# First group of a pooled-attention and gelu MLP kernel: half of K pooled on the PE, w_in in 512 KB pieces cast by GpSimd, gelus over two blocks, and 64x64 score tiles for the remainder rows

## The chip, the cores and the metric

The kernel runs on 1 core of one Trainium2 chip. The metric is the device time in microseconds (us) of one execution; medians over several executions are given. The profile of one execution gives a span, from the first to the last instruction, that is shorter than the device time of that execution: by 2.00 to 2.18 us in every run of the kernel before and of what was built from it (299.3 against 301.36 us), but by only 1.67 to 1.79 us in every run of the changed kernel and of what was built from that. So spans are compared with spans and times with times; the result comes back to these 0.3 us.

In the profile's lines PE is TensorE (PEld its weight loads), DVE VectorE, ACT ScalarE, POOL GpSimd and SPq the queue that issues the loads. Of the tiles, kv holds the loaded K and V, sc the scores, e their exponentials, r the reciprocals of the sums, eb the attention weights (e times r; this step is called the norm), tp a transpose, xo the values, xT the MLP's input. w_in_s is the loaded float32 w_in, w_in_b its bfloat16 cast, mm the MLP's result in PSUM, the memory that TensorE writes to, and gT the gelus.

## The reference

```python
def _attn_ref(q, k, v):                      # each (8, 8, 576, 64) float32
    B, H, S, D = q.shape
    pool = 8
    Sp = S // pool                           # 72
    k_p = k.reshape(B, H, Sp, pool, D).mean(axis=3)
    v_p = v.reshape(B, H, Sp, pool, D).mean(axis=3)
    scores = (1 / sqrt(D)) * matmul(q, k_p.T)
    attn = softmax(scores)                   # over the 72 pooled keys
    return matmul(attn, v_p)

def _moe_ref(x, w_in, w_out):                # x (4608, 512), w_in (512, 2048), w_out (2048, 512)
    h = x @ w_in
    g = gelu_tanh(h)
    return g @ w_out
```

The attention output, with its heads side by side, is x. All inputs and the output are float32.

## The kernel before

The rows are worked in nine groups of 512: 512 rows of each batch entry, and one "remainder" group R with the last 64 rows of all eight. A group's MLP is 64 hidden matmuls (w_in is stationary, columns of xT move) with a gelu for each block of 128, then 64 output matmuls. The attention of the next group is slipped in between these matmuls by "hooks", numbered by the matmul ahead of which they stand. In the first group nothing can hide the attention or the loads: it works in two halves of 256 rows, in chunks of four blocks of 128 (one chunk needs 1 MB of w_in).

```python
    def pool(b, c0, c1):                     # eight rows summed on VectorE
        ...
        add(out=t[:, :, 0:4, :], in0=t[:, :, 0:4, :], in1=t[:, :, 4:8, :], op=ALU.add)
        add(out=t[:, :, 0:2, :], in0=t[:, :, 0:2, :], in1=t[:, :, 2:4, :], op=ALU.add)
        add(out=kvb[:, c0:c1, 0, :], in0=t[:, :, 0, :], in1=t[:, :, 1, :], op=ALU.add)

    def pool_v_pe(b, c0, c1, eng):           # or eight matmuls with the identity, in fp32
        ps = psum.tile([128, 2, D], F32, name="vp", tag="mm", bufs=4)
        for i in range(8):
            nc.tensor.matmul(out=ps, lhsT=identf, rhs=st[b]["kv"][:, c0:c1, i, :], start=(i == 0), stop=(i == 7))
        copy(eng, st[b]["kvb"][:, c0:c1, 0, :], ps)
    ...
    def scores(g, j):
        ...
            else:                            # group R: two batch entries share a block of 128 rows
                for half in range(2):
                    p0 = 64 * half
                    nc.tensor.matmul(out=o[p0:p0 + 64], lhsT=qT[:, j, pr, p0:p0 + 64],
                                     rhs=kbd[:, 2 * j + half, pr].rearrange("d hh s -> d (hh s)"),
                                     start=True, stop=True)
    ...
    def hidden(g, fo, c0, c1, hook, s):
        hp = psum.tile([128, MAIN], F32, name="mm", tag="mm", bufs=4)
        for ko in range(KO):
            hook(s + ko)
            nc.tensor.matmul(out=hp[:, 0:c1 - c0], lhsT=w_in_b[:, ko, fo * 128:(fo + 1) * 128],
                             rhs=st[g]["xT"][:, ko, c0:c1], start=(ko == 0), stop=(ko == KO - 1))
        nc.scalar.activation(out=gT[:, fo, c0:c1], in_=hp[:, 0:c1 - c0], func=ACT.Gelu_apprx_tanh)
    ...
        for half, c in [(0, 0), (0, 1), (0, 2), (0, 3), (1, 0), (1, 1), (1, 2), (1, 3)]:   # the first group
            for fo in range(4 * c, 4 * c + 4):
                hidden(g, fo, 256 * half, 256 * half + 256, hook, s)
                s += 4
    ...
    warm_up(44, "mm")                        # filler matmuls for the TensorE clock
    kT_tile(0, "mm")
    pool(0, 0, 2)
    dup_k(0, 0, 2)
    k_transpose_pe(0, 0, 2)
    pool(0, 2, 4)
    dup_k(0, 2, 4)
    warm_up(22, "mm")
    k_transpose_pe(0, 2, 4)
    ...
    norm(0, 2, nc.gpsimd)                    # block 2 of the first group: its multiply on GpSimd
    cast_w_in(1, nc.vector)                  # w_in was loaded in four pieces of 1 MB
    norm(0, 3, nc.vector)
    cast_w_in(2, nc.gpsimd)
```

The softmax here doesn't subtract the row's maximum and nothing guards it: scores larger than these inputs give would overflow.

Of the kernel before, what the change touches and what calls it, by code (L numbers as in the profile page):

```python
# [19 lines left out]
def kernel(  # L20
# [100 lines left out]

    def pool(b, c0, c1):
        if "kvb" not in st[b]:
            st[b]["kvb"] = work.tile([128, NB, 2, D], BF16, name="kvb")
        t = st[b]["kv"][:, c0:c1]
        kvb = st[b]["kvb"]
        add = nc.vector.tensor_tensor
        add(out=t[:, :, 0:4, :], in0=t[:, :, 0:4, :], in1=t[:, :, 4:8, :], op=ALU.add)  # L128
        add(out=t[:, :, 0:2, :], in0=t[:, :, 0:2, :], in1=t[:, :, 2:4, :], op=ALU.add)  # L129
        add(out=kvb[:, c0:c1, 0, :], in0=t[:, :, 0, :], in1=t[:, :, 1, :], op=ALU.add)  # L130

    def pool_v_pe(b, c0, c1, eng):

        ps = psum.tile([128, 2, D], F32, name="vp", tag="mm", bufs=4)
        for i in range(8):
            nc.tensor.matmul(out=ps, lhsT=identf, rhs=st[b]["kv"][:, c0:c1, i, :], start=(i == 0), stop=(i == 7))
        copy(eng, st[b]["kvb"][:, c0:c1, 0, :], ps)

# [63 lines left out]
    def scores(g, j):  # L202
        sc = psum.tile([128, 2, MAIN], F32, name="sc", tag="sc", bufs=2)
        qT = st[g]["qT"]
        for pr in range(HP):
            o = sc[:, pr // 2, 2 * Sp * (pr % 2):2 * Sp * (pr % 2) + 2 * Sp]
            if g < B:
                nc.tensor.matmul(out=o, lhsT=qT[:, j, pr, :], rhs=kbd[:, g, pr].rearrange("d hh s -> d (hh s)"),  # L208
                                 start=True, stop=True)
            else:  # L210
                for half in range(2):
                    p0 = 64 * half
                    nc.tensor.matmul(out=o[p0:p0 + 64], lhsT=qT[:, j, pr, p0:p0 + 64],  # L213
                                     rhs=kbd[:, 2 * j + half, pr].rearrange("d hh s -> d (hh s)"),
                                     start=True, stop=True)
        st[g][("sc", j)] = sc
# [8 lines left out]
    def norm(g, j, eng):  # L225
        e = st[g][("e", j)]
        den = work.tile([128, H], F32, name="den")
        nc.vector.reduce_sum(out=den, in_=e, axis=AX.X)  # L228
        r = work.tile([128, H], F32, name="r")
        nc.vector.reciprocal(out=r, in_=den)  # L230
        eng.tensor_tensor(out=eb[:, j, 128 * 5 - W:].rearrange("p (h s) -> p h s", s=Sp), in0=e,  # L231
                          in1=r.unsqueeze(2).to_broadcast([128, H, Sp]), op=ALU.mult)

    def eT_tile(g):
        st[g]["eT"] = work.tile([128, 4, 5, 128], BF16, name="eT", bufs=1)

    def e_transpose_pe(g, j, eng):
        tp = psum.tile([128, 5, 128], BF16, name="tp", tag="mm", bufs=4)
        for c in range(5):
            nc.tensor.transpose(out=tp[:, c, :], in_=eb[:, j, 128 * c:128 * c + 128], identity=identb)  # L240
        copy(eng, st[g]["eT"][:, j], tp)
# [6 lines left out]

    def values_half(g, half, x, eng):

        xo = psum.tile([128, 2, 256], F32, name="xo", tag="mm", bufs=4)
        for i in range(2):
# [38 lines left out]

    def hidden(g, fo, c0, c1, hook, s):
        hp = psum.tile([128, MAIN], F32, name="mm", tag="mm", bufs=4)
        for ko in range(KO):
            hook(s + ko)
            nc.tensor.matmul(out=hp[:, 0:c1 - c0], lhsT=w_in_b[:, ko, fo * 128:(fo + 1) * 128],  # L296
                             rhs=st[g]["xT"][:, ko, c0:c1], start=(ko == 0), stop=(ko == KO - 1))
        nc.scalar.activation(out=gT[:, fo, c0:c1], in_=hp[:, 0:c1 - c0], func=ACT.Gelu_apprx_tanh)  # L298

# [9 lines left out]
    def mlp(g, hooks, last):  # L309
        hook = runner(hooks)  # L310
        for fo in range(FO):
            hidden(g, fo, 0, MAIN, hook, 4 * fo)
        if not last:
# [21 lines left out]
    def mlp_first(g, hooks):  # L335

        hook = runner(hooks)
        s = 0
        for half, c in [(0, 0), (0, 1), (0, 2), (0, 3), (1, 0), (1, 1), (1, 2), (1, 3)]:
            for fo in range(4 * c, 4 * c + 4):  # L340
                hidden(g, fo, 256 * half, 256 * half + 256, hook, s)
                s += 4
        nc.scalar.preload_act_table_set(EXP_SET)
# [28 lines left out]
    w_in_s = []  # L372
    for c in range(2):
        t = kvp.tile([128, KO, 1024], F32, name="w_in_s", tag="kv")
        w_in_s.append(t)
        for i in range(2):
            nc.sync.dma_start(
                out=t[:, :, 512 * i:512 * i + 512],
                in_=moe_w_in[:, 1024 * c + 512 * i:1024 * c + 512 * i + 512].rearrange("(ko p) f -> p ko f", p=128))

    def cast_w_in(c, eng):
        o = 512 * c
        copy(eng, w_in_b[:, :, o:o + 512], w_in_s[c // 2][:, :, 512 * (c % 2):512 * (c % 2) + 512])

# [7 lines left out]

    def cast_w_out(c, eng):
        copy(eng, w_out_b[:, 4 * c:4 * c + 4, :], w_out_s[c // 2][:, 4 * (c % 2):4 * (c % 2) + 4, :])

    make_identity(nc, identb)
    nc.vector.memset(kbd, 0.0)
    nc.gpsimd.memset(vmask, 0.125)  # L398
# [5 lines left out]
    nc.gpsimd.memset(vbd[0:64, :, 0, :], 0.0)  # L404
    make_identity(nc, identf)

# [5 lines left out]

    warm_up(44, "mm")
    kT_tile(0, "mm")
    pool(0, 0, 2)
    dup_k(0, 0, 2)
    k_transpose_pe(0, 0, 2)
    pool(0, 2, 4)
    dup_k(0, 2, 4)
    warm_up(22, "mm")  # L420
    k_transpose_pe(0, 2, 4)
    pool(0, 4, 5)
    dup_k(0, 4, 5)
    warm_up(22, "mm")
    k_transpose_pe(0, 4, 5)
    k_spread(0, [nc.vector, nc.scalar])
    qT_tile(0)
    eT_tile(0)
    xT_tile(0)
    warm_up(12, "mm")  # L430
    cast_q(0, 0, 1, nc.vector)
    cast_q(0, 1, 2, nc.scalar)
    q_transpose_pe(0, 0, nc.vector, "mm")
    q_transpose_pe(0, 1, nc.scalar, "mm")
    warm_up(4, "sc")
    for j in range(2):
# [3 lines left out]
    spread_v(0, nc.gpsimd, (0,))  # L440
    pool_v_pe(0, 7, 9, nc.scalar)
    spread_v(0, nc.gpsimd, (1,))
    cast_q(0, 2, 4, nc.gpsimd)
    spread_v(0, nc.gpsimd, (2,))
    warm_up(8, "mm")
    norm(0, 0, nc.vector)
    norm(0, 1, nc.vector)
    e_transpose_pe(0, 0, nc.scalar)
    q_transpose_pe(0, 2, nc.scalar, "mm")
    q_transpose_pe(0, 3, nc.scalar, "mm")  # L450
    e_transpose_pe(0, 1, nc.vector)
    cast_w_in(0, nc.vector)
    scores(0, 2)
    exps(0, 2)
    values_half(0, 0, 0, nc.vector)
    scores(0, 3)
    exps(0, 3)
    values_half(0, 0, 1, nc.scalar)
    nc.scalar.preload_act_table_set(GELU_SET)
    norm(0, 2, nc.gpsimd)  # L460
    cast_w_in(1, nc.vector)
    norm(0, 3, nc.vector)
    cast_w_in(2, nc.gpsimd)

    def first_t(j):
        e_transpose_pe(0, j, nc.vector)

    def first_v():
        cast_w_in(3, nc.vector)
        values_half(0, 1, 0, nc.scalar)  # L470
        values_half(0, 1, 1, nc.vector)

# [7 lines left out]
    for c in range(4):  # L480
        w_out_load(c)
    load_main(1, "v", 0, 4, nc.sync)

# [20 lines left out]
    at(hooks, 32, first_t, 3)  # L504
    at(hooks, 42, first_v)
    at(hooks, 66, pool, 1, 0, 4)
    at(hooks, 66, dup_k, 1, 0, 4)
    at(hooks, 66, pool, 1, 4, 5)
    at(hooks, 66, dup_k, 1, 4, 5)
    at(hooks, 80, cast_q, 1, 0, 2, nc.vector)  # L510
    at(hooks, 80, cast_q, 1, 2, 4, nc.vector)
    at(hooks, 96, kT_tile, 1, "sc")
    at(hooks, 96, qT_tile, 1)
    at(hooks, 96, k_transpose_pe, 1, 0, 5)
    at(hooks, 96, k_spread, 1, [nc.vector, nc.vector])
    for j in range(4):
        at(hooks, 104 + 6 * j, q_transpose_pe, 1, j, nc.vector, "sc")
    at(hooks, 122, eT_tile, 1)
    at(hooks, 122, cast_w_out, 0, nc.vector)
    at(hooks, 122, cast_w_out, 1, nc.gpsimd)  # L520
    for j in range(4):
        at(hooks, [126, 127, 136, 140][j], scores, 1, j)
        at(hooks, [128, 128, 136, 140][j], exps, 1, j)
        at(hooks, [136, 140, 144, 148][j], norm, 1, j, nc.vector)
        at(hooks, [136, 140, 144, 148][j], e_transpose_dma, 1, j)
    at(hooks, 141, cast_w_out, 2, nc.scalar)
    at(hooks, 141, cast_w_out, 3, nc.scalar)
    for i in range(2):
        at(hooks, 160, pool, 1, 5 + 2 * i, 7 + 2 * i)
        at(hooks, 160, spread_v, 1, nc.gpsimd, (0, 1) if i == 0 else (2,))  # L530
    at(hooks, 150, q_tile, 2)
    at(hooks, 150, load_q, 2, 0, 4, nc.sync)
    at(hooks, 150, load_kv, 2)
    tail_of_attention(hooks, 1, 187)
    mlp_first(0, hooks)

    for n_, g in enumerate(seq):
# [3 lines left out]
        if n_ + 1 < len(seq):  # L541
# [7 lines left out]
            if kv:  # L549
                t0 = 20 if n_ == 1 else 12  # L550
                at(hooks, t0, pool, b, 0, 5)
# [58 lines left out]
```

## Time and profile before

| | kernel before |
|---|---|
| median of the device time | 301.14 us (300.91 to 301.18) |
| span of the profile | 299.3 us |
| first hidden matmul | 19.26 us |
| first output matmul of the first group | 38.70 us |
| first hidden matmul of the second group | 54.94 us |
| a later group | 30.4 us |

The prediction below shows the page's chain, the two largest groups, the stage windows and PE's waits. What it doesn't show is the chain in order of time (start, us, what), which is the best measure for a comparison, since it has the matmuls whose records are missing filled in:

```profile
20.25 2.09 POOL eb L231
22.34 0.05 issue
22.38 0.45 PE tp L240 x5
22.83 1.75 PE mm L296 x16
...
55.11 13.81 PE mm L296 x64
...
221.33 0.37 PE sc L213 x8
```

The reader should see three marks: GpSimd's multiply on the chain at 20.25, the second group's hidden matmuls from 55.11 (their first record starts at 54.94; the chain is 0.17 later), and a score set of the remainder group of 0.37 us (there are four).

### The profile page before, as it was taken

The page shows a single profiled execution, that of the slowest core. Times are in us where ns is not written, and L with a number is a line of the kernel's source. Part 1 is how long each engine was busy: PE and PEld are TensorE (multiplying, and loading weights), DVE is VectorE, ACT ScalarE, POOL GpSimd, SP SyncE. Part 2 cuts the span into 40 slices and gives each one's busy share as a digit, 9 for nine tenths or more (in the row PEclk, how much of TensorE's full clock was granted, in tenths as well). Part 3 has the DMA queues.
Part 4 walks back from the last instruction along what each step waited for, and adds up shares of the span by engine and source line. Part 5 has one row for each costly group of instructions (what it writes and reads, how often), then busy time and mean ns, then how long its engine had stood idle before and what let it go on. Part 6 is the DMA issues. An engine that isn't in the chain of part 4 may idle for free.

```text
span 299.3 us, 4581 instructions
## 1 busy us (share of the span) xinstructions
PE 290.7 (97%) x1734; PEld 151.6 (51%) x1734; DVE 146.7 (49%) x241; ACT 158.2 (53%) x242; POOL 55.5 (19%) x71
## 2 busy tenths in 40 slices
PE   7869999999999999999999999999999999999996
PEld 7748844445444544454445444544444544444444
DVE  6895769164706570648073807381639100920012
ACT  1477783667157715672477246724773267426500
POOL 3252033230400240024012400240024000100000
PEclk9999999999999999999999999999999999999999
DMA  7999997995699459947993599049944800351012
GB/s 235 357 387 338 384 350 132 343 279 158 135 279 250 145 127 271 269 146 126 261 297 134 119 249 301 4 107 249 276 147 101 164 36 2 79 114 37 0 70 70
DMA packets 73221, 56.32 MB, mean 188 GB/s; under 512 B 45808, under 2 KB 55408, under 8 KB 73200
## 3 DMA queue, kind: packets, MB, share of 16 engines
q1 hardware_dynamic: 73056, 55.98, 68.2%
q8 instruction: 13, 0.21, 0.3%
q10 hardware_dynamic: 144, 0.07, 0.1%
q14 instruction: 8, 0.07, 0.1%
HBM read 36.70 MB, written 9.44 MB: 154 GB/s over the span
## 4 chain that ended last, share of the span: by engine, by line
PE 91%; DMA 3%; DVE 2%; SPq 1%; POOL 1%; issue 0%; POOLq 0%
PE mm L296 41%; PE mm L301 41%; PE xo L266 4%; DMA q_sb<-in_q_dram 3%; PE sc L208 2%; PE mm L329 1%; POOL eb L231 1%; SPq L98 1%; PE xo L272 1%; PE tp L193 1%; PE sc L213 0%; DVE w_in_b L80 0%; PE tp L240 0%; DVE w_out_b L80 0%; POOL q_b L80 0%; PE xo L255 0%
## 5 line engine op out<-in xcount | busy, mean ns | idle before, releaser
L301 PE MATMUL mm<-w_out_b,gT 128*128 128x512 bf16 x560 | 128.6, 379 | 0.5 <-DVE w_out_b L80 0.5
L296 PE MATMUL mm<-xT,w_in_b 128*128 128x512 bf16 (+1 forms) x640 | 127.6, 358 | 0.5 <-DVE xT L80 0.5
L298 ACT ACTIVATE gT<-mm 128x512 bf16<-128x512 f32 (+1 forms) x160 | 88.4, 555 | 47.0 <-PE mm L296 45.9
L296 PEld LDWEIGHTS <-w_in_b 128*128 128x128 bf16 x640 | 62.2, 98 | 62.6 <-issue 0.5
L301 PEld LDWEIGHTS <-gT 128*128 128x128 bf16 x560 | 53.4, 98 | 59.7 <-DVE w_out_b L80 0.7
L80 DVE COPY osb<-mm 128x512 f32<-128x512 f32 (+2 forms) x37 | 24.3, 658 | 62.9 <-PE mm L301 60.8
L78 ACT CAST xT<-xo 128x1024 bf16<-128x1024 f32 (+1 forms) x18 | 16.6, 966 | 56.8 <-PE xo L266 49.1
L228 DVE TENSOR_REDUCE den<-e 128x8 f32<-128x576 f32 x36 | 26.5, 736 | 38.0 <-ACT e L221 37.9
L148 POOL TENSOR_TENSOR vbd<-kvb,vmask 128x256 bf16<-128x256 bf16 (+2 forms) x40 | 21.2, 553 | 113.5 <-DVE kvb L130 113.4
L128 DVE TENSOR_TENSOR kv<-kv 128x1024 f32<-128x1024 f32 (+3 forms) x20 | 22.4, 1118 | 29.7 <-DMA kv<-in_v_dram 27.7
L231 DVE TENSOR_TENSOR eb<-e,r 128x576 bf16<-128x576 f32 x28 | 27.2, 970 | 1.0
L221 ACT ACTIVATE e<-sc 128x576 f32<-128x576 f32 x36 | 22.5, 650 | 9.6 <-ACT e L221 4.0
L231 POOL TENSOR_TENSOR eb<-e,r 128x576 bf16<-128x576 f32 x8 | 10.1, 1266 | 71.5 <-ACT e L221 41.1
L80 POOL CAST q_b<-q_sb 128x2048 bf16<-128x2048 f32 (+1 forms) x7 | 15.0, 2147 | 4.1 <-DMA q_sb<-in_q_dram 4.1
L208 PEld LDWEIGHTS <-qT 128*128 128x128 bf16 x128 | 10.1, 98 | 7.0 <-ACT qT L78 0.6
L208 PE MATMUL sc<-kbd,qT 128*128 128x144 bf16 x128 | 13.2, 226 | 0.2 <-ACT qT L78 0.2
L266 PE MATMUL xo<-eT,vbd 128*128 128x512 bf16 x56 | 13.2, 379 | 0.0
L129 DVE TENSOR_TENSOR kv<-kv 128x512 f32<-128x512 f32 (+3 forms) x20 | 12.8, 640 | 0.7
L410 PE MATMUL warm<-identb 128*128 128x128 bf16 x112 | 9.1, 249 | 1.4 <-POOL vmask L398 1.4
L494 ACT ACT_TABLE_LOAD x8 | 10.3, 1283 | 0.1
L80 DVE COPY kbd<-kTd 64x288 bf16<-64x288 bf16 x12 | 5.6, 467 | 8.3 <-DMA kTd<-kvb 8.2
L314 ACT ACT_TABLE_LOAD x7 | 9.0, 1283 | 0.1
(55 smaller groups left out, 99.5 us busy)
## 6 DMA issues: line engine op xcount, KB each, us to landing
out_dram<-osb SPq DMA_DIRECT2D x31, 256.0 KB, 6.7
kv<-in_k_dram SPq DMA_DIRECT2D x7, 1024.0 KB, 6.5
q_sb<-in_q_dram SPq DMA_DIRECT2D x7, 1024.0 KB, 5.9
kv<-in_v_dram SPq DMA_DIRECT2D x7, 1024.0 KB, 9.9
w_in_s<-in_moe_w_in_dram SPq DMA_DIRECT2D x4, 1024.0 KB, 13.0
w_out_s<-in_moe_w_out_dram SPq DMA_DIRECT2D x4, 1024.0 KB, 13.8
out_dram<-osb SPq DMA_DIRECT2D x9, 128.0 KB, 2.3
kv<-in_k_dram SPq DMA_DIRECT2D x2, 512.0 KB, 3.9
```

What stands on the lines that cost most here:

```text
L78: eng.copy(out=out, in_=in_)
L80: eng.tensor_copy(out=out, in_=in_)
L128: add(out=t[:, :, 0:4, :], in0=t[:, :, 0:4, :], in1=t[:, :, 4:8, :], op=ALU.add)
L148: eng.tensor_tensor(out=vbd[p0:128, b, n0:n1, :].rearrange("p (c r) (hh d) -> p c (r hh) d", c=max(m, 1), d=D), in0=kvb[p0:128, 4 + c0:4 + ...
L208: nc.tensor.matmul(out=o, lhsT=qT[:, j, pr, :], rhs=kbd[:, g, pr].rearrange("d hh s -> d (hh s)"), start=True, stop=True)
L221: nc.scalar.activation(out=e.rearrange("p (x h) s -> p x (h s)", x=2), in_=sc[:, :, 0:4 * Sp], func=ACT.Exp, scale=1.0 / 64.0)
L228: nc.vector.reduce_sum(out=den, in_=e, axis=AX.X)
L231: eng.tensor_tensor(out=eb[:, j, 128 * 5 - W:].rearrange("p (h s) -> p h s", s=Sp), in0=e, in1=r.unsqueeze(2).to_broadcast([128, H, Sp]), ...
L266: nc.tensor.matmul(out=xo[:, i, :], lhsT=vbd[:, g, n, :], rhs=eT[:, :, c, :], start=(x == 0), stop=(x == 1))
L296: nc.tensor.matmul(out=hp[:, 0:c1 - c0], lhsT=w_in_b[:, ko, fo * 128:(fo + 1) * 128], rhs=st[g]["xT"][:, ko, c0:c1], start=(ko == 0), stop ...
L298: nc.scalar.activation(out=gT[:, fo, c0:c1], in_=hp[:, 0:c1 - c0], func=ACT.Gelu_apprx_tanh)
L301: nc.tensor.matmul(out=o, lhsT=gT[:, fo, r * 128:(r + 1) * 128], rhs=w_out_b[:, fo, :], start=(fo == 0), stop=(fo == FO - 1))
```

## The change

The intent: in the first group, get K pooled sooner by sharing the sums between VectorE and PE; load w_in in half-MB pieces and have GpSimd cast each piece as it lands; give VectorE the norm of block 2 instead; put the first chunk of half 1 ahead of chunk 3 in half 0, so that PE has work while the last MB comes; halve the number of gelus; drop 66 of 112 filler matmuls. Two more parts: q's first cast moves ahead of the spreading of K and the second from ScalarE to GpSimd, and the first half of w_out is cast by GpSimd in five smaller pieces (hook 110), where VectorE and GpSimd cast 1 MB each (hook 122). Outside the first group, the remainder's scores use the array as four 64x64 tiles. Cut to its core (hook numbers, loads of the next group, the casts of w_out, the norm's new layout for group R and buffer tags are left out):

```diff
-    def pool_v_pe(b, c0, c1, eng):
-
+    def pool_pe(b, c0, c1, copies, eng):
+
+        n = c1 - c0
         ps = psum.tile([128, 2, D], F32, name="vp", tag="mm", bufs=4)
         for i in range(8):
-            nc.tensor.matmul(out=ps, lhsT=identf, rhs=st[b]["kv"][:, c0:c1, i, :], start=(i == 0), stop=(i == 7))
-        copy(eng, st[b]["kvb"][:, c0:c1, 0, :], ps)
+            nc.tensor.matmul(out=ps[:, 0:n], lhsT=identf, rhs=st[b]["kv"][:, c0:c1, i, :], start=(i == 0), stop=(i == 7))
+        kvb = st[b]["kvb"]
+        copy(eng, kvb[:, c0:c1, 0:copies, :], ps[:, 0:n].unsqueeze(2).to_broadcast([128, n, copies, D]))
...
+            for hh in range(2):
+                for p0 in (0, 64):
+                    h0 = 64 * hh
+                    nc.tensor.matmul(out=sc[p0:p0 + 64, hh, Sp * pr:Sp * pr + Sp],
+                                     lhsT=qT[h0:h0 + 64, j, pr, p0:p0 + 64],
+                                     rhs=kbd[h0:h0 + 64, 2 * j + p0 // 64, pr, hh], start=True, stop=True)
...
+    def hidden_half(g, fo, half, hook, s):
+
+        c0 = 256 * half
+        hp = psum.tile([128, 2, 256], F32, name="mm", tag="mm", bufs=4)
+        for f in range(2):
+            for ko in range(KO):
+                hook(s + 4 * f + ko)
+                nc.tensor.matmul(out=hp[:, f, :], lhsT=w_in_b[:, ko, (fo + f) * 128:(fo + f + 1) * 128],
+                                 rhs=st[g]["xT"][:, ko, c0:c0 + 256], start=(ko == 0), stop=(ko == KO - 1))
+        nc.scalar.activation(out=gT[:, fo:fo + 2, c0:c0 + 256], in_=hp, func=ACT.Gelu_apprx_tanh)
...
-        for half, c in [(0, 0), (0, 1), (0, 2), (0, 3), (1, 0), (1, 1), (1, 2), (1, 3)]:
-            for fo in range(4 * c, 4 * c + 4):
-                hidden(g, fo, 256 * half, 256 * half + 256, hook, s)
-                s += 4
+        for half, c in [(0, 0), (0, 1), (0, 2), (1, 0), (0, 3), (1, 1), (1, 2), (1, 3)]:
+            for fo in range(4 * c, 4 * c + 4, 2):
+                hidden_half(g, fo, half, hook, s)
+                s += 8
...
-    for c in range(2):
-        t = kvp.tile([128, KO, 1024], F32, name="w_in_s", tag="kv")
-        w_in_s.append(t)
-        for i in range(2):
+    for c in range(4):
+        if c % 2 == 0:
+            w_in_s.append(kvp.tile([128, KO, 1024], F32, name="w_in_s", tag="kv"))
+        o = 512 * (c % 2)
+        for k0 in (0, 2):
             nc.sync.dma_start(
-                out=t[:, :, 512 * i:512 * i + 512],
-                in_=moe_w_in[:, 1024 * c + 512 * i:1024 * c + 512 * i + 512].rearrange("(ko p) f -> p ko f", p=128))
-
-    def cast_w_in(c, eng):
-        o = 512 * c
-        copy(eng, w_in_b[:, :, o:o + 512], w_in_s[c // 2][:, :, 512 * (c % 2):512 * (c % 2) + 512])
+                out=w_in_s[-1][:, k0:k0 + 2, o:o + 512],
+                in_=moe_w_in[128 * k0:128 * k0 + 256, 512 * c:512 * c + 512].rearrange("(ko p) f -> p ko f", p=128))
+
+    def cast_w_in(c, k0, eng):
+        o = 512 * (c % 2)
+        copy(eng, w_in_b[:, k0:k0 + 2, 512 * c:512 * c + 512], w_in_s[c // 2][:, k0:k0 + 2, o:o + 512])
...
-    warm_up(44, "mm")
+    kvb_tile(0)
+    qT_tile(0)
+    eT_tile(0)
+    xT_tile(0)
+    warm_up(34, "mm")
     kT_tile(0, "mm")
     pool(0, 0, 2)
     dup_k(0, 0, 2)
+    pool_pe(0, 2, 4, 2, nc.scalar)
     k_transpose_pe(0, 0, 2)
-    pool(0, 2, 4)
-    dup_k(0, 2, 4)
-    warm_up(22, "mm")
-    k_transpose_pe(0, 2, 4)
     pool(0, 4, 5)
     dup_k(0, 4, 5)
-    warm_up(22, "mm")
     k_transpose_pe(0, 4, 5)
+    k_transpose_pe(0, 2, 4)
+    cast_q(0, 0, 1, nc.vector)
     k_spread(0, [nc.vector, nc.scalar])
-    qT_tile(0)
-    eT_tile(0)
-    xT_tile(0)
-    warm_up(12, "mm")
-    cast_q(0, 0, 1, nc.vector)
-    cast_q(0, 1, 2, nc.scalar)
+    cast_q(0, 1, 2, nc.gpsimd)
+    warm_up(4, "sc")
     q_transpose_pe(0, 0, nc.vector, "mm")
     q_transpose_pe(0, 1, nc.scalar, "mm")
-    warm_up(4, "sc")
     for j in range(2):
         scores(0, j)
         exps(0, j)
     pool(0, 5, 7)
     spread_v(0, nc.gpsimd, (0,))
-    pool_v_pe(0, 7, 9, nc.scalar)
+    pool_pe(0, 7, 9, 1, nc.scalar)
     spread_v(0, nc.gpsimd, (1,))
-    cast_q(0, 2, 4, nc.gpsimd)
+    cast_q(0, 2, 3, nc.gpsimd)
     spread_v(0, nc.gpsimd, (2,))
-    warm_up(8, "mm")
     norm(0, 0, nc.vector)
     norm(0, 1, nc.vector)
-    e_transpose_pe(0, 0, nc.scalar)
+    e_transpose_pe(0, 0, nc.scalar, "mm")
+    cast_q(0, 3, 4, nc.scalar)
+    cast_w_in(0, 0, nc.gpsimd)
+    warm_up(8, "sc")
+    e_transpose_pe(0, 1, nc.vector, "mm")
     q_transpose_pe(0, 2, nc.scalar, "mm")
     q_transpose_pe(0, 3, nc.scalar, "mm")
-    e_transpose_pe(0, 1, nc.vector)
-    cast_w_in(0, nc.vector)
-    scores(0, 2)
-    exps(0, 2)
-    values_half(0, 0, 0, nc.vector)
-    scores(0, 3)
-    exps(0, 3)
-    values_half(0, 0, 1, nc.scalar)
+    cast_w_in(0, 2, nc.vector)
+    for x in range(2):
+        values_half(0, 0, x, [nc.vector, nc.scalar][x], "mm")
+    for j in (2, 3):
+        scores(0, j)
+        exps(0, j)
     nc.scalar.preload_act_table_set(GELU_SET)
-    norm(0, 2, nc.gpsimd)
-    cast_w_in(1, nc.vector)
+    norm(0, 2, nc.vector)
     norm(0, 3, nc.vector)
-    cast_w_in(2, nc.gpsimd)
+    for c in range(1, 4):
+        cast_w_in(c, 0, nc.gpsimd)
+        cast_w_in(c, 2, nc.gpsimd)
```

## The prediction

The sum is -1.45 + 0.15 = -1.3 us, giving 299.8 and, with something for the landings, 299.6; its +0.15 was the estimate for the remainder's scores. In step (3), the 1.2 us of a cast beside VectorE's work was an estimate; half of the 2.33 us that GpSimd's cast of 128x2048 took beside VectorE's cast of w_out (alone 1.93) comes to 1.17. Rival B keeps the wait; the causes that it gave, GpSimd's order of work among them, are cut with the delay of 0.5 to 1 us.

> **What bounds the kernel now.** I read the page first. Its chain that ended last, and the costliest two groups:
>
> ```profile
> PE 91%; DMA 3%; DVE 2%; SPq 1%; POOL 1%; issue 0%; POOLq 0%
> L301 PE MATMUL mm<-w_out_b,gT 128*128 128x512 bf16 x560 | 128.6, 379 | 0.5 <-DVE w_out_b L80 0.5
> L296 PE MATMUL mm<-xT,w_in_b 128*128 128x512 bf16 (+1 forms) x640 | 127.6, 358 | 0.5 <-DVE xT L80 0.5
> ```
>
> The chain is 91% PE, so only what lies before or between matmuls can be won. Second view, the windows: before the first hidden matmul, hidden phase of the first group, its output phase, one later group (columns: stretch, length, then busy us of each engine with its count, clock, DMA share, GB/s).
>
> ```profile
> 0.00:19.26 19.26, 15.36 (x183) 13.50 (x184) 14.78 (x29) 7.66 (x13) 6.86 (x19) 1.00 0.95 316
> 19.26:38.70 19.44, 17.75 (x176) 15.43 (x175) 14.71 (x27) 14.09 (x36) 4.64 (x3) 1.00 1.06 367
> 38.70:54.94 16.24, 16.20 (x80) 7.56 (x81) 11.67 (x21) 10.32 (x10) 4.75 (x6) 1.00 0.88 248
> 54.94:85.50 30.56, 30.56 (x154) 14.39 (x153) 14.54 (x25) 17.31 (x26) 7.92 (x8) 1.00 0.84 217
> ```
>
> A later group has no PE gap at all. The hidden phase of the first group loses 19.44 - 17.75 = 1.69 us, the output phase 0.04. Before 19.26 PE works on the attention and on filler. So the change can win only a start before 19.26, those 1.69 us, and what it does to the remainder group's scores. The third view, PE's waits in the first 60 us, names the 1.69 (total, times, longest); the timeline shows what stood behind:
>
> ```profile
> PE tp L240 <- POOL eb L231: 1.2, 1, 1.2
> PE mm L301 <- DVE w_out_b L80: 0.5, 1, 0.5
> ...
> 17.38 1.23 DVE L80 CAST w_in_b<-w_in_s 128x2048 bf16<-128x2048 f32 x1
> 18.53 0.68 DVE L80 CAST xT<-xo 128x512 bf16<-128x512 f32 x1
> 20.25 2.08 POOL L231 TENSOR_TENSOR eb<-e,r 128x576 bf16<-128x576 f32 x1 [3.07 <-DVE r L230]
> 22.83 1.93 POOL L80 CAST w_in_b<-w_in_s 128x2048 bf16<-128x2048 f32 x1 [0.51 <-DMA w_in_s<-in_moe_w_in_dram]
> 25.52 1.23 DVE L80 CAST w_in_b<-w_in_s 128x2048 bf16<-128x2048 f32 x1
> ```
>
> The reader should see two things. GpSimd's multiply of 2.08 us holds the transposes at 22.38. And the casts start when their data land: in the view of tile w_in_s,
>
> ```profile
> L377 SPq DMA_DIRECT2D w_in_s<-in_moe_w_in_dram x4: 1827/1955/2387, 5.4 to 11.3; - x4
> DMA to landing us min/median/max: 11.9/13.0/14.2
> ```
>
> issue plus landing gives 5.4 + 11.9 = 17.3 for the first MB and 11.3 + 14.2 = 25.5 for the last, so one MB each 2.7 us (17.4, 20.1, 22.8, 25.5), with the DMA share at 0.95 to 1.06: **the load of w_in is a second bound, close behind PE**.
>
> [...] VectorE's multiply eb<-e,r took 0.82 us at 13.31 but 1.29 us at 15.06 beside GpSimd, and GpSimd's cast of 128x2048 took 1.93 us alone, 2.33 us beside VectorE's cast of w_out. [...] 44 filler matmuls took 4.45 us from 1.43, the next 22 only 1.39. [...] the trace has 0.42 us of weight-load idle before each set of eight 128x64 score matmuls, and 0.37 us for the set. [...] gelu of 256 columns 385 ns, of 512 about 600.
>
> **The change part by part.**
> (1) K's middle half goes from VectorE to PE: VectorE loses 0.68 + 0.42 + 0.29 + 0.20 = 1.6 us. PE gains eight fp32 matmuls, 2.0 us by the V half that PE already pools; ScalarE a copy of 256 columns, about 0.35. VectorE is done with K at about 7.6 instead of 8.64. But K's transposes of that half wait for landing 5.75 (read from the trace's landing times) + 2.0 + 0.35 = 8.2, and q's first half lands only at 8.6. Scores start near 9.9 instead of 11.14: 1.2 us won, but not yet at the end.
> (2) That lead is then lost to data. q's second half lands at 14.65 in both kernels, and gates the transposes of q; w_in's first MB is complete at 17.36. VectorE now casts only half of it, 0.65 us, done at 18.0; its copy of xT (0.68) follows in order: first hidden matmul near 18.7. **Won at the start: 0.5 us.**
> (3) Seven of eight half-MB casts are GpSimd's, 0.97 us each (half of 1.93), a piece landing each 1.35 us, so it keeps up[...]. The norm of the third block moves to VectorE: e at 18.8, eb at about 20.6 to 21.0. Chunk 0 of hidden work is 16 x 0.11 = 1.76 us, until 20.5, so the wait of 1.19 shrinks to some 0.3. Chunk 1 is cast at 20.07 + 1.2 = 21.3; PE needs it at about 21.3. Chunk 2 is cast at 22.78 + 1.1 = 23.9; PE needs it at 21.3 + 1.76 + 0.45 (transposes) = 23.5. Chunk 3, at 26.6, is now needed only after the first chunk of half 1, at about 28.4: no wait.
> (4) So the landing of chunk 2 sets the phase. From 23.9: rest of chunk 2 1.76, values 1.04, five chunks 8.8, K transposes 0.35, q transposes 4 x 0.22: end 36.75. Before, outputs began at 38.70 after two scores (0.5) that now fall into the output phase: compare with 38.2. **Won in all up to the outputs: 38.2 - 36.75 = 1.45 us**, the 0.5 of (2) included.
> (5) w_out lands in the same order behind the same DMA load (first MB 35.3, then each 2.7 us); GpSimd casts its first 128x512 piece by 35.9, before 36.75. Later pieces: fo 4 needed at 40.7, ready 39; fo 8 needed near 44.6, ScalarE's casts start near 42.3. No wait. V of the next group lands by 46.04, is pooled on VectorE by 49, spread by 49.7; its values come near 50.7. No wait, 1 us spare.
> (6) Gelus over two blocks: ScalarE 16 x 0.60 = 9.6 instead of 32 x 0.385 = 12.3 us, not on the chain: 0.
> (7) Remainder group scores: per block 16 matmuls of 64x64 by 72 columns for 8 of 128x64 by 144. [...]
> Sum: -1.45 + 0.15 = -1.3, giving 299.8; since the author may gain something from smaller landings, I take **299.6 us**.
>
> **The rivals.**
> A. Landings improve: half-MB pieces complete earlier than now because less later data runs ahead of them. For it: by the page's queue rates about 0.9 MB more than its own had moved when each MB landed. Against: total bytes and rate are unchanged. Worth up to 1 us at chunk 2: 298.5.
> B. A new wait takes the place: [...] PE waits for GpSimd's w_in_b instead of eb. For it: seven casts beside VectorE's norms. Against: 0.97 us per 1.35. It makes 300.3 to 301.
> C. The clock: fillers fall from 112 to 46 matmuls, so PE could fall back to half clock before 19 us. For it: PE would be thin between 13.9 and 15.4. Against: the pooling matmuls fill 2 us each[...]. It would cost about 1.7 us: 301.5.
> D. The remainder's scores truly run four at a time, 0.2 us a set, and win 0.7: 299.0.
>
> **Range and chances.** A ceiling: w_in's chunk 2 can't be in before 22.78, so over 2 us needs A or D; over 2% is 6 us, more than the whole idle of the first group's hidden phase and its lead together. A loss of 2% needs the clock and a new wait at once. I predict 299.6, range 298.0 to 300.9, faster 0.02, same 0.97, slower 0.01.
>
> **What would show it.** Right: first hidden matmul at 18.4 to 19, outputs from about 36.8, PE's wait for eb gone or under 0.4, a wait for GpSimd's w_in_b of 0.2 to 0.8 in its place, the next group from about 53.5, later groups unchanged at 30.4 us. Wrong: landings of w_in before 22.3 for its third MB (A), a wait over 1 us on GpSimd (B), matmuls at half rate after 6 us (C), a set of remainder scores far from 0.4 us (D, step 7), or a wait for w_out_b or V (step 5).

## More of the kernel before

One more line of the timeline matters later: VectorE's cast of the first MB of w_out, for which PE waits 0.50 us ahead of the first output matmul at 38.70.

```profile
37.42 1.22 DVE L80 CAST w_out_b<-w_out_s 128x2048 bf16<-128x2048 f32 x1
```

## The result

The changed kernel takes **298.9 us** (298.62 to 299.35, 4 runs) against 301.13 us (300.91 to 301.18) in the same rounds. Ratios are computed as the mean time of one kernel's runs over that of the other's of the same rounds, so they are not quite the ratio of the medians: 0.9929, 95% interval 0.9912 to 0.9946. By the 2% rule that is "same". The change gains 0.7%, and lies within the predicted range, with more gain than the 299.6 predicted.

The page of the changed kernel has the same kind of chain; VectorE's 2% are gone, and the loads (DMA) and their issue (SPq) have 3% more. After it, the windows of the same four stages (stretch, length, busy us with count of PE, weight loads, VectorE, ScalarE, GpSimd, then clock, DMA share, GB/s):

```profile
PE 91%; DMA 4%; SPq 3%; POOL 1%; issue 0%; DVE 0%
```

```profile
0.00:17.57 17.57, 13.46 (x133) 11.53 (x134) 12.53 (x24) 6.66 (x12) 8.38 (x21) 1.00 0.94 309
17.57:36.70 19.13, 17.74 (x175) 15.01 (x173) 11.47 (x24) 12.05 (x21) 10.16 (x10) 1.00 1.06 368
36.70:52.98 16.28, 16.28 (x87) 7.80 (x85) 11.68 (x22) 10.89 (x13) 5.55 (x8) 1.00 1.01 293
52.98:83.36 30.38, 30.38 (x154) 14.29 (x153) 14.51 (x23) 17.43 (x26) 7.91 (x8) 1.00 0.83 216
```

Hidden work starts 19.26 - 17.57 = 1.69 us sooner; the hidden phase is 19.44 - 19.13 = 0.31 us shorter; the output phase is 0.04 us longer: 1.96 us in all, which is what the second group's start shows (54.94 to 52.98). The hidden phase still idles 19.13 - 17.74 = 1.39 us, nearly the 1.69 of before: the waits were exchanged, not removed. PE's waits (total, times, longest) name the new ones:

```profile
PE tp L254 <- DVE eb L240: 1.5, 2, 0.8
...
PE mm L321 <- POOL w_in_b L80: 0.7, 2, 0.5
```

The first line is 0.79 us ahead of the hidden phase and 0.69 inside it; with the second line's 0.7 that makes the 1.39. The chain in order of time has the rest:

```profile
10.77 10.40 DMA w_in_s<-in_moe_w_in_dram
21.16 0.05 issue
21.21 2.59 POOL w_in_b L80 x2
23.80 0.05 issue
23.85 0.61 PE mm L321 x4
...
53.15 13.83 PE mm L310 x64
...
219.51 0.25 PE sc L220 x16
```

The load of w_in (the first half of chunk 2 landed at 21.16), two casts on GpSimd and then PE: this is the path that sets the first group's end now. And a score set of the remainder group takes 0.25 us instead of 0.37, in all four sets 4 x 0.12 = 0.48 us. By the chain: 55.11 - 53.15 = 1.96, plus 0.48, makes 2.44 us, and the spans differ by 299.3 - 296.9 = 2.4. So the difference of these two profiles is accounted for; what is left to find is which part of the change made the 1.96.

It is not quite the difference of the times. The profiled run of the kernel before (301.36 us) is slower than its timed ones, that of the changed kernel (298.62) the fastest of its four. The medians differ by 2.23 us; 0.3 of these lie outside the span, where every run of the changed kernel has less (only 1.67 to 1.79 us), and which part of the change does that stays open. Within the span a usual run gains about 1.9 (299.1 against 297.2).

### The profile page after: what moved, and what is told of

Its sections match the earlier page's. It is cut to its first block, busy times and chain, and to the rows that moved or that the text cites. A ratio compares the mean times of both kernels' runs of the same rounds, so it can differ in the third digit from the quotient of the medians. Undisturbed runs are those within 1.5% of the kernel's fastest.

```text
span 296.9 us, 4533 instructions
## 1 busy us (share of the span) xinstructions
PE 288.5 (97%) x1716; PEld 149.3 (50%) x1716; DVE 140.3 (47%) x234; ACT 155.9 (52%) x229; POOL 63.3 (21%) x82
## 3 DMA queue, kind: packets, MB, share of 16 engines
HBM read 36.70 MB, written 9.44 MB: 155 GB/s over the span
## 4 chain that ended last, share of the span: by engine, by line
PE 91%; DMA 4%; SPq 3%; POOL 1%; issue 0%; DVE 0%
PE mm L326 41%; PE mm L310 37%; PE xo L280 4%; PE mm L321 4%; DMA w_in_s<-in_moe_w_in_dram 4%; PE sc L213 2%; SPq L403 2%; PE mm L354 1%; POOL w_in_b L80 1%; SPq L98 1%; PE xo L286 1%; SPq L110 0%; PE sc L220 0%; PE tp L198 0%; PE xo L269 0%
## 5 line engine op out<-in xcount | busy, mean ns | idle before, releaser
L310 PE MATMUL mm<-xT,w_in_b 128*128 128x512 bf16 x512 | 111.8, 379 | 0.0
L312 ACT ACTIVATE gT<-mm 128x512 bf16<-128x512 f32 x128 | 76.5, 597 | 41.8 <-PE mm L310 41.8
L131 DVE TENSOR_TENSOR kv<-kv 128x1024 f32<-128x1024 f32 (+3 forms) x19 | 21.8, 1147 | 33.8 <-DMA kv<-in_v_dram 30.0
L240 DVE TENSOR_TENSOR eb<-e,r 128x576 bf16<-128x576 f32 x26 | 24.4, 940 | 0.9
L80 POOL CAST q_b<-q_sb 128x2048 bf16<-128x2048 f32 (+2 forms) x9 | 17.1, 1897 | 14.6 <-DMA q_sb<-in_q_dram 8.5
L240 POOL TENSOR_TENSOR eb<-e,r 128x576 bf16<-128x576 f32 x6 | 6.9, 1149 | 61.3 <-ACT e L228 34.1
L321 PE MATMUL mm<-xT,w_in_b 128*128 128x256 bf16 x128 | 15.9, 273 | 0.7 <-POOL w_in_b L80 0.7
L323 ACT ACTIVATE gT<-mm 128x512 bf16<-128x512 f32 x16 | 9.4, 597 | 5.2 <-PE mm L321 5.2
## 6 DMA issues: line engine op xcount, KB each, us to landing
kv<-in_v_dram SPq DMA_DIRECT2D x4, 512.0 KB, 10.2
```

The source lines that it names most:

```text
L80: eng.tensor_copy(out=out, in_=in_)
L240: eng.tensor_tensor(out=o.rearrange("p (h s) -> p h s", s=Sp), in0=e, in1=r.unsqueeze(2).to_broadcast([128, H, Sp]), op=ALU.mult)
L310: nc.tensor.matmul(out=hp, lhsT=w_in_b[:, ko, fo * 128:(fo + 1) * 128], rhs=st[g]["xT"][:, ko, :], start=(ko == 0), stop=(ko == KO - 1))
L312: nc.scalar.activation(out=gT[:, fo, :], in_=hp, func=ACT.Gelu_apprx_tanh)
L321: nc.tensor.matmul(out=hp[:, f, :], lhsT=w_in_b[:, ko, (fo + f) * 128:(fo + f + 1) * 128], rhs=st[g]["xT"][:, ko, c0:c0 + 256], start=(ko ...
```

## The experiments

Twelve kernels ran, in three sets; each set was on one chip with its own runs of the kernel before. Ratios are to the kernel before of the same rounds.

| run | median, us | ratio, 95% interval | second group starts at, us (one profile) |
|---|---|---|---|
| changed kernel | 298.90 | 0.9929 (0.9912 to 0.9946) | 52.98 |
| r_undo | 299.82 | 0.9951 (0.9939 to 0.9963) | 53.36 |
| r_only | 300.68 | 0.9983 (0.9971 to 0.9995) | 55.00 |
| k_undo | 299.04 | 0.9930 (0.9917 to 0.9943) | 53.42 |
| w_in_1mb | 299.84 | 0.9953 (0.9941 to 0.9965) | 54.14 |
| control (changed kernel again) | 298.62 | 0.9915 (0.9902 to 0.9928) | 53.20 |
| warm_44 | 299.24 | 0.9930 (0.9918 to 0.9941) | 53.10 |
| c2_best | 298.79 | 0.9924 (0.9911 to 0.9937) | 53.20 |
| norm2_pool | 301.70 | 1.0014 (0.9993 to 1.0035) | 56.85 |
| few_fill | 301.43 | 1.0023 (0.9996 to 1.0049) | 54.53 |
| gelu_undo | 310.08 | 1.0300 (1.0284 to 1.0315) | 64.28 |
| less_w_in (wrong result) | 298.87 | 0.9926 (0.9913 to 0.9939) | 52.85 |
| best | 299.25 | 0.9937 (0.9925 to 0.9949) | 53.19 |

The last column is the start of the second group's first hidden matmul (54.94 in the kernel before). It shows the first group alone: after it, chance stalls of PE of up to 0.6 us come in some executions, in groups that the change doesn't touch (below), and they blur the times. Two profiles of the same kernel, the changed kernel and control, differ in it by 0.22 us.

### The remainder's scores: r_undo and r_only

r_undo takes the old score matmuls and norm of group R into the changed kernel, r_only the new ones into the kernel before:

```diff
-                continue
-            for hh in range(2):
-                for p0 in (0, 64):   # sixteen 64x64 matmuls of 72 columns
+            else:
+                for half in range(2):   # eight 128x64 matmuls of 144 columns
```

> The changed kernel with the old scores and norm of the remainder group (eight 128x64 matmuls a block instead of sixteen 64x64). The profile of the changed kernel has 0.25 us for each of the four score sets where the kernel before has 0.37. Theory (the scores gave 0.48 of the gain): 298.9 + 0.5 = 299.4 us, the set back at 0.37. Rival (all of the gain is from the first group): 298.9, no difference.

> The kernel before with only the new remainder scores and their norm. Theory: 301.13 - 0.5 = 300.65 us, everything up to the remainder group unchanged to 0.05 us. Rival: 301.1.

r_only is the clean one: its ratio of 0.9983 is -0.51 us of 301.24, where -0.5 was expected, and its second group starts at 55.00, as before (54.94). Its score sets take 0.25 us, and those of r_undo 0.37:

```profile
L215 PE MATMUL sc<-kbd,qT x64: 195/196/217, 221.3 to 225.8; 64*64 64x72 bf16 x64
```

A single matmul's record is 196 ns long, but a set of sixteen advances the chain by 0.25 us, 16 ns each: the four tiles do overlap (in the trace of the changed kernel's first set, four matmuls start 3 to 4 ns apart, the next four 22 to 43 ns later). r_undo lost more than the 0.48: (0.9951 - 0.9929) x 301 = 0.7 us; the rest lies within the intervals. In its profile, of the slowest of its six runs, group R takes 31.40 us instead of 30.94, and two later groups 30.86 and 30.99 instead of 30.35, each with one wait of PE (0.35 and 0.48 us): chance stalls, not the scores.

### K on the PE: k_undo

```diff
-    pool_pe(0, 2, 4, 2, nc.scalar)
+    pool(0, 2, 4)
+    dup_k(0, 2, 4)
+    warm_up(22, "mm")
```

> The changed kernel with K's middle half pooled on VectorE again, with the 22 filler matmuls of before in place of the pooling matmuls. Theory L (from chunk 2 of w_in on, loading and casting set the phase, whatever came before): scores 1 us later, first hidden matmul about 18.4 to 18.8 instead of 17.57, but outputs within 0.3 us of the changed kernel, 298.9 to 299.2 us. Rival K (the time won on K is the gain): about 1.1 us slower, 300.0 us.

299.04 us, ratio 0.9930 against 0.9929. In its profile the first hidden matmul is at 18.92 instead of 17.57, so the start was lost, and PE's wait at chunk 2 is there as in the changed kernel:

```profile
18.92 1.91 PE L321 MATMUL mm<-xT,w_in_b 128*128 128x256 bf16 x16 [1.18 <-DVE xT L80]
...
24.19 0.61 PE L321 MATMUL mm<-xT,w_in_b 128*128 128x256 bf16 x4 [0.48 <-POOL w_in_b L80]
```

The changed kernel's PE went on at 23.85, so of the 1.35 us lost at the start 0.34 reach chunk 2 (outputs began at 37.13, 0.43 later than the changed kernel's and 0.22 later than control's), and in the times nothing measurable does: the difference of the ratios is 0.0001, with an uncertainty of some 0.002, or 0.6 us. Rival K falls: **pooling half of K on the PE, the part that names the change, is worth nothing that these runs can measure.**

But the start was not lost for the reason that theory L gives, scores 1 us later. They came at 10.13, against 10.02 in the changed kernel and 11.14 in the kernel before (PE's timeline of k_undo, 5 to 10.5 us):

```profile
10.13 0.42 PE L213 MATMUL sc<-kbd,qT 128*128 128x144 bf16 x4
```

VectorE was done with K at 8.68, when q had only just landed (8.61). So 1.0 of the 1.1 us that the scores gained come from something else than K; few_fill, the kernel before with fewer fillers, has its first scores at 10.81; for the rest the timelines suggest q's earlier casts (no run undoes them). What delayed the first hidden matmul to 18.92 was the load: the second half of w_in's first MB landed at 17.55 instead of 15.85, the first load to land after the packet on the instruction queue that is told under "The fillers and the load".

### The pieces of w_in: w_in_1mb

```diff
-        for k0 in (0, 2):      # two loads of 512 KB
-            nc.sync.dma_start(out=w_in_s[-1][:, k0:k0 + 2, o:o + 512], ...)
+        nc.sync.dma_start(out=w_in_s[-1][:, :, o:o + 512], ...)   # one of 1 MB, same casts
```

> The changed kernel with w_in loaded in four pieces of 1 MB as before, all casts as in the changed kernel. Theory L: the two halves of chunk 2 then come together at about 22.6, GpSimd casts them one after the other (2 x 1.04) and PE gets chunk 2 at 24.7 instead of 23.85: about 0.9 us slower, 299.8 us, and the first chunk lands near 17.3 again. Rival (pieces only change when the first hidden matmul starts, and that is lost anyway): 298.9 to 299.1 us.

299.84 us: 0.8 us slower than k_undo of the same set, and by the ratios 0.7 us slower than the changed kernel, near the 0.9 of theory L. GpSimd's timeline shows the reason; two casts start at the landing of each whole MB:

```profile
19.81 2.55 POOL L80 CAST w_in_b<-w_in_s 128x1024 bf16<-128x1024 f32 x2 [2.28 <-DMA w_in_s<-in_moe_w_in_dram]
22.52 2.52 POOL L80 CAST w_in_b<-w_in_s 128x1024 bf16<-128x1024 f32 x2 [0.15 <-DMA w_in_s<-in_moe_w_in_dram]
25.22 1.04 POOL L80 CAST w_in_b<-w_in_s 128x1024 bf16<-128x1024 f32 x1 [0.18 <-DMA w_in_s<-in_moe_w_in_dram]
```

Chunk 2 is cast at 25.04 instead of 23.79 (the 23.80 of the chain above), and the second group starts 1.16 us later. One sub-expectation missed: the first MB landed at 15.86, not near 17.3. So the earlier landing of the first MB (15.85 in the changed kernel, 17.36 before) doesn't come from the pieces; few_fill takes this up.

### The norm of block 2: norm2_pool

```diff
-    norm(0, 2, nc.vector)
+    norm(0, 2, nc.gpsimd)
```

> The changed kernel with the multiply of the third block's norm on GpSimd again, as before. Theory: GpSimd then casts the second MB of w_in 1.3 to 2 us later, and chunk 2 after it, so the phase ends 1 to 1.5 us later: 300.1 us. Rival (only the wait for eb of 0.7 us is touched, and the landing of w_in absorbs it): 299.0 us.

301.70 us, 3 us slower than the control and more than theory and rival had. One of its six runs, at 300.05 us, has a mean granted clock of 1.0; the other five (301.13 to 302.50) have 0.993 or 0.994. The profile's windows show what happened (the first of the last three columns is the clock):

```profile
22.00:24.00 2.00, 0.90 (x7) 0.41 (x7) 1.02 (x2) 0.61 (x2) 2.00 (x2) 0.89 1.05 386
24.00:26.00 2.00, 1.62 (x8) 1.04 (x8) 0.00 (x0) 0.00 (x0) 2.00 (x3) 0.50 1.05 388
```

After PE had waited for GpSimd (1.2 us for eb, then 1.1 for w_in_b until 23.55), the TensorE clock fell to half at 23.6 us and came back at 27.0. So the wait itself seems to cost 300.05 - 298.62 = 1.4 us, as the theory had it, and the fallen clock up to 2.4 us more; the split rests on the single run that kept its clock, and that the waits brought the clock down is read from the order of events. Giving VectorE this multiply, together with w_in's casts on GpSimd, is a part that counts.

### GpSimd or the landing: c2_best and less_w_in

The prediction said that the landing of chunk 2 sets the phase. c2_best takes chunk 2's casts off GpSimd; less_w_in leaves out the load of its second half, and casts the first half a second time in its place (an edit that is not shown):

```diff
c2_best
     def first_t(j):
         e_transpose_pe(0, j, nc.vector, "sc")
+        if j == 2:
+            cast_w_in(2, 0, nc.scalar)
+            cast_w_in(2, 2, nc.vector)
less_w_in
         for k0 in (0, 2):
+            if (c, k0) == (2, 2):
+                continue
```

> The changed kernel with the two casts of chunk 2 taken off GpSimd: the first half on ScalarE, the second on VectorE after the second eT copy. Theory P (GpSimd's cast of chunk 2, held up behind VectorE's multiply for 0.55 us, sets the phase, more than the landing at 22.52): chunk 2 is cast by 23.3, PE's second wait for w_in_b (0.48) goes, about 0.4 us faster than the control. Rival L (the landing sets it): 0.1 us or nothing.

> The changed kernel without the load of the second half of chunk 2 (512 KB less; its cast reads data that is there, so the result is wrong on purpose). Theory P (GpSimd's queue sets chunk 2: its cast of the first half ends at 22.8, after the second half's landing at 22.5): chunk 2 is still cast near 23.8, at most 0.1 us faster than the control. Rival L (the landing sets it, as the prediction has it): chunk 2 cast by 23.3 and 0.3 to 0.5 us faster.

less_w_in: with no second half to wait for, chunk 2 was still cast only at 23.76 against 23.79, and the time is within the changed kernel's. So the landing of the second half does not set chunk 2; **the landing of the first half (21.16) and two casts in a row on GpSimd do**. In the changed kernel the cast of the first half started at its landing and took 1.59 us instead of 1.04, beside VectorE's multiply eb<-e,r (21.15 to 21.91, 0.76 us); that the multiply held it up is read from this overlap, and no run takes it away. The second half, landed at 22.52, started at 22.76:

```profile
L80 POOL CAST w_in_b<-w_in_s x7: 1031/1041/1592, 15.3 to 25.3; 128x1024 bf16<-128x1024 f32 x7
```

(min, median and max of the seven casts, in ns.) c2_best was to win 0.4 us, and did not: 0.9924 against 0.9915 for the control. But in its profile it did not do what it was meant to. Chunk 2 was cast by 24.11 instead of the expected 23.3, because ScalarE came to its cast only at 22.42 (landing 21.02) and VectorE to its own at 23.42. PE had no wait for w_in_b, since this execution was one with a late clock (below): its first hidden matmul came at 18.77, and PE waited for the norm instead:

```profile
PE tp L254 <- DVE eb L240: 2.1, 3, 0.8
```

Its second group still starts at 53.20, like control's. So a second chain, q to scores to norm to eb, may lie close behind the cast chain; that is what the trace suggests, and it isn't shown. What taking chunk 2 off GpSimd would be worth stays open.

### The clock: control and warm_44

In the profiles of r_undo, w_in_1mb, c2_best, norm2_pool and gelu_undo the granted clock rose at 9.7 to 10.8 us (9.7, 9.9, 9.9, 10.6 and 10.8), in those of the changed kernel and of control at 5.0 and 5.4 (the first change in the trace's clock records; the windows print 1.00 ahead of that record, so they don't show the rise). The rate of the matmuls does show it. These are the ones that pool K, in the timeline of PE, first the changed kernel, then r_undo, in which these instructions are the same:

```profile
6.00 2.02 PE L140 MATMUL vp<-kv,identf 128*128 128x128 f32 x16 [0.81 <-DMA kv<-in_k_dram]
```

```profile
5.89 3.75 PE L140 MATMUL vp<-kv,identf 128*128 128x128 f32 x16 [0.65 <-DMA kv<-in_k_dram]
```

With 34 fillers PE is busy from 1.4 to 5.2 us and then idle for 0.6 to 1.1. I took this gap for the cause:

```diff
-    warm_up(34, "mm")
+    warm_up(44, "mm")
```

> The changed kernel again, unaltered, to have it on the same chip as the next three. Expected 298.9 us with a spread of some 0.7 us. In two of the four experiment profiles so far the TensorE clock rose only at 9.9 and 10.6 us instead of 5.0, and the pooling of K took 3.8 us instead of 2.0. If that is chance, this profile may show either.

> The changed kernel with 44 filler matmuls ahead instead of 34, as before. Theory H (34 fillers leave a gap of 0.9 us before the pooling matmuls, so in some executions the clock rises only near 10 us): the clock rises before 8.5 us, the spread of the times shrinks, and the median falls by 0 to 0.3 us. Rival (the late rise is absorbed by the wait for w_in): the same median as the control to 0.1 us.

Control is 298.62 with a spread of 0.5 us; warm_44 is 299.24 (298.55 to 299.38), no faster and with no smaller spread. Its one profile has an early clock (the pooling took 2.00 us), as theory H wants; but the gain is not borne out, ten more fillers do not help. A late clock delays the scores (11.3 to 11.7 us in the five profiles, 10.0 to 10.2 with an early one) and the first hidden matmul (18.8 to 19.2 against 17.5 to 17.7), but need not cost much in the end: c2_best's profiled execution, with a late clock, took 298.70 us, as did control's with an early one, though these are two different kernels.

The gap's length does not tell the early clocks (0.81, 0.64, 1.09 us) from the late ones (0.63 to 0.79). What does is not shown: no run tests what sets the moment of the rise, and it may be chance.

### The fillers and the load: few_fill

Why did q's second half and w_in's first MB land 1.5 us sooner in the changed kernel (13.14 and 15.85, before 14.65 and 17.36)? Not for the pieces. In every trace a packet of 16 KB and about 1.1 us runs on the instruction queue, the first at 11 to 18 us, and one of the next two landings comes 1.1 to 1.7 us late: the packet runs at 11.55 us in the kernel before, at 15.26 in the changed one. The DMA view of the kernel before for 10 to 16 us has it (packets, MB, share):

```profile
q8 instruction: 1, 0.02, 1.2%
```

The landing in question came 3.29 us after the one before it in the kernel before, instead of about 1.8, and 2.60 instead of 1.35 in the changed kernel. The traces suggest what places the packet: the first came after 211 to 244 PE instructions in every run (244 in the kernel before, 216 in the changed kernel), the second 238 to 269 later. If so, the fillers, which are PE instructions, should place it. few_fill is the kernel before with the fillers of the changed one:

```diff
-    warm_up(44, "mm")
+    warm_up(34, "mm")
...
-    warm_up(22, "mm")       # and the second 22; 12 become 4, 4 become none
```

> The kernel before with the fillers of the changed kernel (46 instead of 112 matmuls), nothing else. In the profiles so far one packet of 16 KB on the instruction queue, 1.1 us long, appears each time after some 210 to 240 PE instructions, at 11.6 us in the kernel before and at 15.3 to 15.8 us with fewer fillers, and the landing after it comes 1.3 us late. Theory F (the fillers place that fetch): it moves to about 14 to 15.5 us, q's second half lands at 13.1 instead of 14.65, and w_in's first MB at 15.9 or at 17.4, the last MB at 25.3 as ever; the first hidden matmul about 1 us earlier. The time changes little, 300.6 to 301.2 us, since GpSimd's cast of chunk 2 still ends after 24.3. Rival (the landings moved for the smaller pieces): q still lands at 14.65.

Theory F holds in the landings: q 13.17, first MB 15.88, third 22.40; the packet came even later than I said, at 18.0 us, and the landing after it late (18.60 to 22.40 is 3.8 us, where a MB takes 2.7). The rival falls. The first hidden matmul came at 18.79, 0.5 us earlier and not the expected 1. The time did not gain: 301.43 us with a spread of 300.83 to 304.01. Without K's pooling matmuls PE is thin early on, and in this profile the clock rose only at 13.98 us; the second group started 0.41 us sooner, and one wait of PE in a later group (30.75 us instead of 30.35) took that back. So this accident of the changed kernel is real, but it moves mainly the start, and most of the start is then lost at chunk 2.

### One gelu per block: gelu_undo

```diff
-        nc.scalar.activation(out=gT[:, fo:fo + 2, c0:c0 + 256], in_=hp, ...)
+            nc.scalar.activation(out=gT[:, fo + f, c0:c0 + 256], in_=hp[:, f, :], ...)   # in the loop over f
```

> The changed kernel with one gelu per block of 128 again, 32 of 0.385 us instead of 16 of 0.60. Theory (ScalarE isn't on the chain): the control's 298.6 to 298.9 us. Rival (ScalarE then falls behind, gelus and the copies of xT and w_out come late): 0.5 us or more slower.

310.08 us, 11 us slower, but not for the reason that either theory gives. Two blocks share one PSUM tile, and PE's matmuls for the second block now wait until ScalarE has read the first, each time:

```profile
PE mm L321 <- ACT gT L323: 9.1, 15, 2.4
```

The timeline has one after the other: two gelus from 22.92 take 0.82 us, and PE goes on at 23.79, after 0.47 us of waiting for the gelu. The experiment is spoilt as a test of ScalarE's load. For that only the traces speak: gelus of the first group take 9.4 us instead of 12.0, and in neither kernel does PE's list of waits name a gelu.

### A version to beat both: best

best = k_undo + c2_best, with VectorE's first copy of xT ahead of its cast of w_in.

> The changed kernel with K pooled on VectorE again (with 22 fillers), so that no pooling matmul depends on when the clock rises, with the casts of chunk 2 on ScalarE and VectorE, and with the first copy of xT ahead of the cast of w_in on VectorE. If GpSimd's cast of chunk 2 was what kept the start's gain from reaching the end: 298.2 to 298.4 us with a smaller spread, PE without a wait for w_in_b at chunk 2. If the landing of w_in and the norm's chain hold it as well: 298.6 to 299.0 us.

299.25 us: not better. It has no wait for w_in_b at chunk 2, but chunk 2 was cast only by 24.09, so it is no test of the casts either, and its second group starts where control's does (53.19). In the profiled run a wait of 0.59 us in a later group lost 0.75 us on top. All five runs have a mean clock of 0.994. Without K's pooling matmuls PE idles between 7 and 9 us, and the clock that had risen at 6.1 falls at 9.5 and comes back at 12.9:

```profile
7.00:9.00 2.00, 0.29 (x4) 0.20 (x4) 1.83 (x8) 0.00 (x0) 0.44 (x1) 1.00 1.12 344
9.00:11.00 2.00, 1.80 (x18) 1.36 (x17) 1.51 (x4) 0.81 (x2) 0.63 (x2) 0.63 1.07 366
```

Three of k_undo's five runs have a mean clock below 0.995 too: 8 of 10 runs of these two kernels, against 2 of 35 of the changed kernel and its versions that pool K on the PE (norm2_pool and gelu_undo, with their long waits, left out). So the pooling of K on the PE seems to do one thing after all: it replaces fillers, with useful work, in keeping the clock up. No time shows what that is worth. No version ran that beats the changed kernel.

## Why the prediction was right, and where it was off

- **The bound.** Right: PE, then the first group alone. Later groups are unchanged (30.35 to 30.37 us from first hidden matmul to first hidden matmul in both kernels, but for group R, the last one, 0.1 us shorter, and one chance stall), and 0.31 + 1.69 us come from the first group's hidden phase and the lead.
- **Step 1 (K on the PE).** The time is right, the reason wrong. Scores started at 10.02 for the predicted 9.9 (11.14 before), but with K back on VectorE (k_undo) they start at 10.13. VectorE was not done at 7.6, as the step has it, but at 8.24. "Not yet at the end" is right. The step also missed that the pooling matmuls take 2.0 or 3.75 us, with the clock of that execution.
- **Step 2 (start won 0.5 us).** Off: 1.69 us. The step took "q's second half lands at 14.65 in both kernels" and 17.36 for w_in's first MB. They landed at 13.14 and 15.85, since with fewer fillers the packet on the instruction queue came later, at 15.26 instead of 11.55 us (in few_fill at 18.0, and the same two landed at 13.17 and 15.88). The error cost little, since the surplus went into PE's waits in the hidden phase.
- **Step 3 (waits).** Half right. The wait for eb was to shrink to "some 0.3" and was 0.69, because PE came 1.1 us sooner than the step assumed; that for w_in_b was to be 0.2 to 0.8 and was 0.7. A cast alone took 1.04 us, not 0.97.
- **Step 4 (chunk 2 sets the phase, outputs at 36.75, 1.45 us won).** The times are right: the first output matmul is at 36.70, chunk 2 goes on at 23.85 for the predicted 23.9. For the latter there is luck in it. The step gave one landing, 22.78, plus 1.1 for the cast; what counted was the landing of the first half, 21.16, and two casts, the first lengthened to 1.59 us. The gain to the second group's start was 1.96 us, 0.5 more than the term, and this 0.5 lies in the output phase: 53.5 - 36.75 = 16.75 us predicted, 16.28 measured. The step charged it 0.5 us for two more score sets. But in the kernel before that phase began after PE's wait for w_out_b, and in the chain its first eight output matmuls took 1.90 us and its first score set 0.41; now they take 0.22 us each and 0.25.
- **Step 5 (w_out and V hide).** Right: PE has no such wait in the changed kernel, and its output phase has no idle time.
- **Step 6 (gelus 0).** Not tested cleanly; the traces don't contradict it.
- **Step 7 (remainder's scores +0.15 us).** Wrong in sign: -0.48 us, r_only -0.51. The step's time for each matmul was an estimate that no trace showed, and too long: four tiles work side by side, 0.25 us a set of sixteen, 16 ns each. The prediction had named a set far from 0.4 us as a sign of being wrong. This is most of rival D, at 0.25 a set instead of its 0.2.
- **The sum.** -1.45 + 0.15 should have been -1.96 - 0.48 = -2.44 us for the two profiles. So the two terms erred by 0.5 and 0.6 us in the same direction. The medians differ by 2.23 us, of which 0.3 us lie outside the span, where no step looked; and the 299.6 already held 0.2 us for a gain that it could not name. That the time came so near owes something to luck; the bound and the place of the gain do not.
- **The signs.** Outputs from 36.8, w_in_b's wait and the later groups came as named; the first hidden matmul (17.57 for 18.4 to 19), eb's wait and the next group (52.98 for 53.5) did not.
- **The rivals.** A (landings): 1.5 us at the first MB, 0.26 at chunk 2, and from another cause than the pieces. B (GpSimd's queue): its wait exists, 0.7 us, but the gain of the other parts is larger. C (the clock): its sign came, matmuls at about half rate after 6 us, in five of the experiments' profiles (K's pooling took 3.75 to 3.77 us instead of 2.02); but this came at no cost that c2_best's time shows. D: above.
- **Where the 1.96 us came from.** PE went on with chunk 2 at 23.85 instead of 24.86, with two matmuls more done: 1.2 us. Taking back the norm's engine alone costs 1.4 us and more, taking back the pieces some 0.7, taking back K nothing measurable. These are not additive, as all three act on the same stretch up to chunk 2. About 0.5 us more is PE's wait for w_out_b ahead of the outputs, which is gone: VectorE's cast ended at 38.64 there, and GpSimd's smaller pieces start at 35.02 in the changed kernel. That is read from the traces; no run undid it, nor the new order of the chunks, nor q's casts.

## What to carry to other kernels

When one phase waits for a load and its casts, an earlier start is worth little until the last cast on that path comes earlier (in k_undo 0.34 of 1.35 us reached chunk 2): split the load so that casts start with each piece, and keep any other work off the engine that casts. Count what an engine is fed besides its work: with the 112 fillers of the kernel before the clock rose at 5.28 us, with the 46 of few_fill only at 13.98 (one profile each), but the packet on the instruction queue came at 11.55 instead of 18.0 us, and q's second half landed at 14.65 instead of 13.17. The 64x64 score matmuls were worth spreading over the four tiles of the array (0.25 us a set instead of 0.37), and useful matmuls may be better fillers than fillers (by the clocks of k_undo and best, where 8 of 10 runs have a mean below 0.995 against 2 of 35; not shown in a time). Compare the phase that was changed in the traces too, and not only the whole time, in which chance stalls elsewhere can outweigh it.
